# Wider W_in products, raw W_out blocks stored in batch 0, and one common form for the stretch between batches

## The chip, the cores and the metric

The kernel runs on one core of one Trainium2 chip. The metric is the device time of one execution in microseconds (us). Every profile here is one execution taken by the hardware profiler.

Engines: PE is TensorE (matmuls), PEld its weight loads, DVE is VectorE, ACT is ScalarE, POOL is GpSimd, SP is SyncE, which here only issues transfers (its queue is called SPq in the rows).

## What is computed

```python
def attn(x, state):                    # x [8,8,512,64], state [8,8,32,64]
    scores  = softmax(x @ state.T / 8)     # over the 32 states
    xread   = scores @ state               # [8,8,512,64]
    scores2 = softmax(state @ x.T / 8)     # over the 512 tokens
    sread   = scores2 @ x                  # [8,8,32,64]
    return concat([xread, sread], axis=2)  # 544 rows per batch and head
def moe(x, w_in, w_out):               # x [8*544, 512], w_in [512,2048], w_out [2048,512]
    h = x @ w_in
    g = where(h >= 1, h, where(h <= -1, 0, (h + 1)**2 / 4))
    return g @ w_out
```

## The kernel before

**The algebra.** `xread @ W_in` is `a @ (state @ W_in)`, so for each batch b the kernel first multiplies the states by W_in and then the softmax `a` by that product. W_in and W_out lie in eight chunks c or j of 256 hidden columns. Batches 0 to 7 are the 512 tokens of each batch, "batch 8" is the 256 state rows of all batches together. Each batch runs over steps (b, j), j = 0 to 7; a step makes the hidden values of chunk j and adds the product of the step before to the output sums.

**Precision.** Matmuls of the hidden values run in a reduced format. Each operand is held as a high part (written by ACT) and a low remainder (written by DVE), and three products of parts are summed. The small products `state @ W_in` (line 457, tiles `sw`), the scores (line 234, `sc`) and the read of the tokens (line 408, `sr`) are in plain float32. `rest(b, c)` splits one `sw` product: ACT copies the high part, DVE subtracts (line 1242).

**Batch 0** is ordered by hand in `SEQ`, a list per engine; `Plan` turns the lists into an emission order. In it the weights arrive, are decoded (`low`, `high`, `join`), and W_out is split into `wo[c]` (`part_high`, `part_low`). For c = 3 and up the joined W_out chunk `wf` is also stored to DRAM as `flat` from POOL's queue (line 891). `wf` has two buffers (tag `tmp`), so the next `join` into one waits until the `flat` of that buffer has landed and its split has read it.

**Batch 1** runs in `direct`, with 24 output matmuls of 512 columns per step on four PSUM banks `acc`. Beside it the kernel prepares the seven-product form that batches 2 to 7 use for `g @ W_out`: `fold_whole(c)` stores raw quadrants of `wo[c]` to the DRAM tile `fold` with three transfers from SP (lines 644 to 646) and gets the whole chunk again (an addition on POOL, or a load of `flat`); `fold_sums`, `fold_high` and `fold_low` make sums of quadrants, which go to DRAM from POOL. `load_wide(b, c)` brings both sets back as `wd`.

**The stretch between batches** lies in step (b, 0): the read of batch b's tokens (`read2`, needs the softmax tile `e2` and the tokens `xn`), four `sw` products for chunks (1,2), (3,4), (5,6) and (7, next batch's 0), and the scores of batch b+1. Batch 1 has its own form, `stretch`: its products stand in other PSUM tiles (`mm`, then three on `acc`), the scores wait for the `mm` tile, and the scores stay in PSUM while the softmax of batch 2 is worked on in halves. Batches 2 to 7 use `stretch_between`: `sr` on `acc`, products on `h`, `mm`, `acc`, `acc`, scores on `acc`, parked at once in SBUF by two ACT copies (`park_all`).

**Softmax by columns.** `shuffle` transposes `e2` by way of DRAM (`moved`): one store, then four loads back. Up to batch 2 it is issued from SP.

**Queues.** SP and POOL issue transfers in program order; a transfer that waits for a buffer holds up all behind it on that queue. `later(place, b, j, ...)` puts work at a named place of a step; in the steps of batch 1 the places come in the order half, low, mid, end, last.

Of the kernel before, what the change touches and what calls it, by code (L numbers as in the profile page):

```python
# [8 lines left out]
F32 = mybir.dt.float32  # L9
# [11 lines left out]
NG = 0  # L21
HALVES = (0,)
SPILL = 3
SEQ = {
# [76 lines left out]
def state_exchange_moe(  # L101
# [17 lines left out]
    nc = tc.nc  # L119
    B, P, NT, H, D = x.shape  # L120
    S = NT * P
    NS = 32
    DM = H * D
    NPR = H // 2
# [46 lines left out]

    sb = const.tile([P, B, NPR, NS], F32, name="sb")
    srT = const.tile([P, NPR, B, NS], F32, name="srT")
    w32 = [const.tile([P, NPR, CI], F32, name=f"w32_{c}") for c in range(NC)]
    wo = {}
    rows2 = drams.tile([B, P, P], F32, tag="rows2", bufs=1, name="rows2")

# [267 lines left out]
    def sw_product(items, apart=None, home=None, halves=False):  # L445

        b, c = items[0]
        if apart:
            banks = [apart(f"sw{b}_{c}_{hh}") for hh in range(2)]
        else:  # L450
            pt = ps_mm(f"sw{b}_{c}")
            banks = [pt[:, hh] for hh in range(2)]
        for i, (bi, ci) in enumerate(items):
            for pr in range(NPR):
                for hh in range(2):
                    rows = slice(hh * 64, hh * 64 + 64)
                    nc.tensor.matmul(  # L457
                        banks[hh][pr * NS:(pr + 1) * NS, i * CI:(i + 1) * CI],
                        lhsT=sb[rows, bi, pr], rhs=w32[ci][rows, pr], start=True, stop=True,
                    )  # L460
        w = len(items) * CI
        if b == 0 and c < NH:
            whole = work.tile([P, 1024], F32, tag="wh", name=f"sw{b}_{c}w").rearrange("p (q f) -> p q f", q=2)[:, :, :w]
            sw_of[b, c] = [(banks[q][:, :w], whole[:, q], None) for q in range(2)]
            chunk[b, c] = whole, None
            return
        wh, wl = (
            v[:, :2 * w].rearrange("p (q f) -> p q f", q=2) for v in split_tiles(f"sw{b}_{c}", home)
        )
        if apart or halves:  # L470
            sw_of[b, c] = [(banks[q][:, :w], wh[:, q], wl[:, q]) for q in range(2)]
        else:
            sw_of[b, c] = [(pt[:, :, :w], wh, wl)]
        for i, item in enumerate(items):
            cols = slice(i * CI, (i + 1) * CI)
            chunk[item] = wh[:, :, cols], wl[:, :, cols]
# [151 lines left out]
    fold = {}  # L628
    flat = {}

    def fold_whole(c):

        w = wo[c]
        wa = (wop if c >= SPILL else rawp).tile([P, 8, 256], F32, tag="wo" if c >= SPILL else "raw", name=f"wa{c}")
        fold[c] = wa
        hi, lo = (w[:, i].rearrange("p a c -> p (a c)") for i in range(2))
        whole = wa[:, 0:4].rearrange("p a c -> p (a c)")
        if c >= SPILL:
            nc.gpsimd.dma_start(out=whole, in_=flat[c])
        else:  # L640
            nc.gpsimd.tensor_tensor(out=whole, in0=hi.bitcast(F32), in1=lo.bitcast(F32), op=ALU.add)
        kept = folded[c] = drams.tile([P, 2, 8, 256], F32, tag="fold", name=f"fold{c}")
        w4 = w.bitcast(F32).rearrange("p i a (h c) -> p i (a h) c", h=2)
        nc.sync.dma_start(out=kept[:, :, 0:1], in_=w4[:, :, 0:1])
        nc.sync.dma_start(out=kept[:, :, 1:3], in_=w4[:, :, 2:4])
        nc.sync.dma_start(out=kept[:, :, 7:8], in_=w4[:, :, 1:2])

    def fold_sums(c):
        wa = fold[c]
# [265 lines left out]
    def part_low(c):  # L915
        wh, wl = (wo[c][:, i].rearrange("p a c -> p (a c)") for i in range(2))
        nc.vector.tensor_tensor(out=wl, in0=parts[c], in1=wh.bitcast(F32), op=ALU.subtract)

# [226 lines left out]
    def attention(b):  # L1145

        def at(place, j, *names):
            for name in names:
                f, *q = name.split()
                later(place, b - 1, j, (lambda f=f, q=q: getattr(atts[b], f)(*map(int, q)),))  # L1150

        if b == 2:
            at("mid", 1, "turn 0", "turn 1")
            at("low", 2, "top2 0", "top2 1")
            at("mid", 2, "top1 0", "top1 1")
            at("low", 3, "exp2 0", "exp2 1")
            at("mid", 3, "less1 0", "less1 1")
            at("low", 4, "exp1 0", "exp1 1", "turn_blocks 0")
            at("mid", 4, "sum1 0", "inv1 0")
            at("low", 5, "turn_blocks 1", "shuffle")  # L1160
            at("mid", 5, "sum1 1", "inv1 1", "norm1 0")
            at("low", 6, "norm1 1", "back 0")
            at("mid", 6, "back 1", "high1 0", "high1 1", "rest 0")
            at("low", 7, "rest 1")
            return
        at("f2", 1, "turn_all")
        at("f1", 2, "top2_all")
        at("f2", 2, "top1_all", "exp2 0")
        at("f0", 3, "exp2 1")
        at("f1", 3, "less1_all")  # L1170
        at("f2", 3, "exp1 0", "blocks_all")
        at("f0", 4, "exp1 1")
        at("f1", 4, "shuffle", "sum1_all")
        at("f2", 4, "norm1_all")
        at("f1", 5, "back_all")
        at("f2", 5, "high1 0")
        at("f0", 6, "high1 1")
        at("f1", 6, "rest_all")
# [28 lines left out]
    for c in range(2, NJ):  # L1207
        later("half", 1, c - 1, (fold_whole, c))
        later("low", 1, c, (fold_high, c - 1))
        later("mid", 1, c, (fold_low, c - 1))  # L1210
    later("end", 1, 2, (load_later, 0))
    later("mid", 1, 7, (one, 0, "read2", "scale2"))
    later("mid", 3, 5, (one, 0, "place2"))
    later("mid", 4, 5, (one, 1, "place2"))
# [4 lines left out]
    later("end", 1, 7, (fold_high, 7), (fold_low, 7))  # L1219
    for c in range(NG):  # L1220
        later("mid", 1, 0, (part_late, c))
    for c, (b, j) in enumerate(((1, 7), (1, 7), (1, 7))):
        later("last", b, j, (load_wide, 2, c))
    order = [s for s in steps if s[0] > 1]
    for i, s in enumerate(order[3:]):
# [15 lines left out]
            nc.scalar.copy(out=wh, in_=pt)  # L1241
            nc.vector.tensor_tensor(out=wl, in0=pt, in1=wh.bitcast(F32), op=ALU.subtract)  # L1242

    def stretch(b):
        atts[b].read2()
        sw_product([(b, 1), (b, 2)], halves=True)
        sw_product([(b, 3), (b, 4)], ps_acc)
        sw_product([(b, 5), (b, 6)], ps_acc, "xn")
        rest(b, 1)
        att_start(b + 1)  # L1250
        rest(b, 3)
        sw_product([(b, 7), (b + 1, 0)], ps_acc, "raw")
        atts[b].scale2()
        rest(b, 5)
        rest(b, 7)

    def stretch_between(b, now):

        final = b + 1 == B
        atts[b].read2(ps_acc)  # L1260
        atts[b].scale2()
        sw_product([(b, 1), (b, 2)], ps_h)
        rest(b, 1)
        if not final:
            att_start(b + 1, apart=ps_acc)
            atts[b + 1].park_all()
        now.last_sums()
        sw_product([(b, 3), (b, 4)])
        rest(b, 3)
        now.high(1)  # L1270
        now.low(1)
        now.high(2)
        sw_product([(b, 5), (b, 6)], ps_acc, "xn")
        rest(b, 5)
        now.low(2)
        sw_product([(b, 7), (b + 1, 0)][:1 if final else 2], ps_acc, "raw")

    def direct(b, j, prior):
        hid = g1(b, j, split=False)
# [18 lines left out]
    def sevenfold(b, j, prior, before):  # L1298
        now = Seven(b, j)
        old = before if before else None  # L1300
        gather = Gather(prior[0]) if old and j == 0 else None
        first = j == 0 and b < B
        late = old and old.b < B and old.j > 0
        now.product(0)
        now.curve(0)
        if late:
            old.high(2)
        now.bound(0)
        issue("curved", b, j)
        now.first_sum()  # L1310
        if late:
            old.low(2)
        issue("f0", b, j)
        now.high(0)
        now.low(0)
        issue("f1", b, j)
        if old:
            old.outer(0)
        else:
            g2(*prior, 0)  # L1320
        if gather:
            gather.keep(1)
            gather.keep(7)
            gather.add(2)
        issue("mid", b, j)
        now.product(1)
        now.curve(1)
        if old:
            old.outer(1)
        else:  # L1330
            g2(*prior, 1)
        if gather:
            gather.add(6)
            gather.keep(4)
        now.bound(1)
        if gather:
            gather.add(5)
            gather.keep(3)
            joins(gather, b)
        if first:  # L1340
            stretch_between(b, now)
        else:
            now.high(1)
            now.last_sums()
            now.low(1)
            issue("f2", b, j)
        return now
# [28 lines left out]
    with guard:  # L1376
        plan.emit(warm)
        before = None
        for i, (b, j) in enumerate(steps):
# [8 lines left out]
            if j == 1 and b + 2 < B:  # L1388
                loaded["xt", b + 2] = load_xt(b + 2)
            issue("end", b, j)  # L1390
            if j == 6 and b + 1 < B:
                loaded["xn", b + 1] = load_xn(b + 1)
            issue("last", b, j)
        g2(*steps[-1])
# [43 lines left out]
```

## Time and profile before

| | |
|---|---|
| median of 3 runs | 629.36 us (628.64 to 630.17) |
| profiled execution | 631.39 us, span of its work 629.5 us |
| busy, share of the span | PE 614.4 us (98%), DVE 499.3 (79%), ACT 464.4 (74%), POOL 66.4 (11%) |
| DMA | 178.05 MB, mean 283 GB/s |
| PE clock granted | full in all slices |

How to read it: the span runs from the first to the last instruction; the execution is 1.9 us longer. A matmul's end is modelled and overlaps the next one's start, so time on PE is best read from start to start. "Issue" as the releaser of a wait means that the profile shows no semaphore that the engine waited for.

### The profile page before, as it was taken

The numbers are of one execution on the slowest core, as the hardware profiler recorded it, in microseconds if no ns is written. First come the engines' busy times: TensorE is split into PE (matmuls) and PEld (weight loads), VectorE is DVE, ScalarE is ACT, GpSimd is POOL, SyncE is SP. The second block draws the span as 40 slices with busy tenths as digits, with TensorE's granted clock in tenths as the row PEclk, the third lists the DMA queues.
The fourth block names the chain that finished last, engine by engine and source line by source line (L and its number), as shares of the span: only waits on it lengthen the run. The fifth ranks groups of instructions, "written<-read, shape, count | busy, mean of one in ns | idle before, by whom it ended". The sixth has DMA issues, their size and how long they took to land.

```text
span 629.5 us, 12904 instructions
## 1 busy us (share of the span) xinstructions
PE 614.4 (98%) x5154; PEld 531.8 (84%) x5154; DVE 499.3 (79%) x765; ACT 464.4 (74%) x746; POOL 66.4 (11%) x85
## 2 busy tenths in 40 slices
PE   8999999999889999999999999999999999999997
PEld 3577776888679997999889998999899988999995
DVE  6999978799579878897789877997789777678631
ACT  6998855766478778787788777877878777777642
POOL 0000201211100101201120102010121011000200
PEclk9999999999999999999999999999999999999999
DMA  8993469869999987989698979999788978998741
GB/s 350 415 415 156 124 250 334 309 241 346 341 414 362 303 302 226 284 314 312 231 315 274 333 295 282 275 343 320 234 231 317 297 252 220 263 376 268 230 121 34
DMA packets 56715, 178.05 MB, mean 283 GB/s; under 512 B 9424, under 2 KB 25424, under 8 KB 53712
## 3 DMA queue, kind: packets, MB, share of 16 engines
q1 hardware_dynamic: 44240, 151.21, 67.2%
q0 software_dynamic: 12080, 25.69, 15.7%
q8 instruction: 41, 0.67, 0.4%
q10 hardware_dynamic: 336, 0.33, 0.2%
q14 instruction: 18, 0.15, 0.1%
HBM read 137.89 MB, written 33.03 MB: 272 GB/s over the span
## 4 chain that ended last, share of the span: by engine, by line
PE 75%; DVE 5%; DMA 4%; issue 2%; ACT 2%; SPq 1%; DVEq 0%; ACTq 0%
PE p L777 13%; PE p L779 13%; PE p L778 13%; PE h L708 7%; PE h L709 7%; PE h L710 7%; PE sw L457 4%; PE acc L612 2%; PE acc L610 2%; PE acc L611 2%; DMA moved<-eb 2%; PE h L523 2%; PE h L522 2%; PE h L524 2%; DMA fold<-wo 1%
## 5 line engine op out<-in xcount | busy, mean ns | idle before, releaser
L729 DVE SCALAR_TENSOR_TENSOR sums<-sums,over 128x512 f32<-128x512 f32 x96 | 65.9, 687 | 57.0 <-ACT sums L725 56.2
L777 PE MATMUL p<-wd,gh 128*128 128x256 f32 x384 | 108.5, 283 | 0.5 <-DVE sw_3l L1242 0.5
L778 PE MATMUL p<-wd,gh 128*128 128x256 f32 x384 | 108.7, 283 | 0.0
L779 PE MATMUL p<-wd,gl 128*128 128x256 f32 x384 | 108.6, 283 | 0.0
L750 ACT CAST gh<-sums 128x512 fp32r<-128x512 f32 x96 | 59.9, 624 | 57.6 <-DVE sums L729 33.3
L723 ACT ACTIVATE sums<-h,half 128x512 f32<-128x512 f32 x96 | 66.3, 691 | 25.7 <-PE h L710 24.2
L779 PE MATMUL p<-wd,gc 128*128 128x256 f32 x288 | 81.6, 283 | 0.0
L777 PE MATMUL p<-wd,gc 128*128 128x256 f32 x288 | 81.6, 283 | 0.0
L778 PE MATMUL p<-wd,gc 128*128 128x256 f32 x288 | 81.5, 283 | 0.0
L777 PEld LDWEIGHTS p<-wd,gh 128*128 128x128 f32 x384 | 72.9, 190 | 4.7 <-DVE sw_3l L1242 0.9
L778 PEld LDWEIGHTS p<-wd,gh 128*128 128x128 f32 x384 | 72.9, 190 | 3.8
L779 PEld LDWEIGHTS p<-wd,gl 128*128 128x128 f32 x384 | 72.9, 190 | 0.0
L754 DVE TENSOR_TENSOR gl<-sums,gh 128x512 fp32r<-128x512 f32 x96 | 65.8, 685 | 4.8 <-ACT gh L750 4.8
L724 ACT ACTIVATE over<-h,less_one 128x512 f32<-128x512 f32 x96 | 65.6, 684 | 0.0
L725 ACT ACTIVATE sums<-sums 128x512 f32<-128x512 f32 x96 | 60.8, 633 | 0.0
L777 PEld LDWEIGHTS p<-wd,gc 128*128 128x128 f32 x288 | 54.9, 191 | 0.0
L779 PEld LDWEIGHTS p<-wd,gc 128*128 128x128 f32 x288 | 54.9, 190 | 0.0
L778 PEld LDWEIGHTS p<-wd,gc 128*128 128x128 f32 x288 | 54.9, 191 | 0.0
L539 ACT ACTIVATE u<-h,half 128x512 f32<-128x512 f32 x40 | 27.0, 686 | 33.4 <-PE h L524 22.8
L612 PE MATMUL acc<-wo,gl 128*128 128x512 f32 x128 | 50.1, 391 | 0.5 <-DVE gl L572 0.5
L610 PE MATMUL acc<-wo,gh 128*128 128x512 f32 x128 | 50.2, 392 | 0.0
L611 PE MATMUL acc<-wo,gh 128*128 128x512 f32 x128 | 49.9, 390 | 0.0
(268 smaller groups left out, 1464.8 us busy)
## 6 DMA issues: line engine op xcount, KB each, us to landing
wd<-fold SPq DMA_DIRECT2D x96, 896.0 KB, 8.0
xt<-in_xt_dram SPq DMA_DIRECT2D x16, 512.0 KB, 8.3
raw_i<-in_moe_w_in_dram SPq DMA_DIRECT2D x8, 1024.0 KB, 9.6
raw_o<-in_moe_w_out_dram SPq DMA_DIRECT2D x8, 1024.0 KB, 12.3
out_dram<-o SPq DMA_DIRECT2D x32, 256.0 KB, 6.9
fold<-wa POOLq DMA_DIRECT2D x8, 1024.0 KB, 7.6
xn<-in_x_dram SPq DMA_DIRECT2D x7, 1024.0 KB, 6.1
fold<-wo SPq DMA_DIRECT2D x16, 256.0 KB, 6.6
```

The costliest lines, as they stand in the source:

```text
L610: nc.tensor.matmul(a, lhsT=lh, rhs=oh, start=f == 0, stop=False)
L611: nc.tensor.matmul(a, lhsT=lh, rhs=ol, start=False, stop=False)
L612: nc.tensor.matmul(a, lhsT=ll, rhs=oh, start=False, stop=f == NF - 1)
L723: nc.scalar.activation(out=g, in_=h, func=AF.Relu, scale=0.5, bias=half)
L724: nc.scalar.activation(out=r, in_=h, func=AF.Relu, scale=1.0, bias=less_one)
L725: nc.scalar.activation(out=g, in_=g, func=AF.Square)
L729: nc.vector.scalar_tensor_tensor(out=g, in0=g, scalar=1.0, in1=r, op0=ALU.min, op1=ALU.add)
L750: nc.scalar.copy(out=gh, in_=s)
L754: nc.vector.tensor_tensor(out=gl, in0=s, in1=gh.bitcast(F32), op=ALU.subtract)
L777: nc.tensor.matmul(o, lhsT=gh[:, sl], rhs=wh, start=opens, stop=False)
L778: nc.tensor.matmul(o, lhsT=gh[:, sl], rhs=wl, start=False, stop=False)
L779: nc.tensor.matmul(o, lhsT=gl[:, sl], rhs=wh, start=False, stop=closes)
```

## The change

1. Chunks 1 and 2, 3 and 4, 5 and 6 of W_in are kept in one tile per pair (`twins`). A product of two such chunks is then one matmul of 512 columns per head pair and half instead of two of 256.
2. The three transfers that store the raw quadrants of `wo[c]` become `keep_raw(c, queue)`. For c = 0 to 4 they are emitted in batch 0, behind `part_low(3)`, `part_low(4)` and `part_low(5)`, on POOL's queue. For c = 5 to 7 they stay in `fold_whole` on SP.
3. Batch 1's stretch takes the form of the later ones, and batch 2's softmax works on the parked scores in whole instructions, its `shuffle` at step (1,3) instead of (1,5).
4. The tokens `xn` of batch 2 are loaded into the `wh`/`wl` buffers at the end of step (1,4), not into `xn` at the end of (1,6).
5. The third pair of `wd` loads is emitted at the end of step (2,0) instead of (1,7).
6. In the last stretch (batch 7) `scale2` and `last_sums` come behind the split of chunks (3,4).

```diff
+RAW = {3: (0,), 4: (1, 2), 5: (3, 4)}
...
-    w32 = [const.tile([P, NPR, CI], F32, name=f"w32_{c}") for c in range(NC)]
+    w32 = [const.tile([P, NPR, CI], F32, name="w32_0")]
+    twins = {}
+    for c in range(1, NC - 1, 2):
+        twins[c] = const.tile([P, 2, NPR, CI], F32, name=f"w32_{c}")
+        w32 += [twins[c][:, i] for i in range(2)]
+    w32.append(const.tile([P, NPR, CI], F32, name=f"w32_{NC - 1}"))
...
+        if c in twins and len(items) == 2:
+            for pr in range(NPR):
+                for hh in range(2):
+                    rows = slice(hh * 64, hh * 64 + 64)
+                    nc.tensor.matmul(
+                        banks[hh][pr * NS:(pr + 1) * NS].rearrange("p (a f) -> p a f", a=2),
+                        lhsT=sb[rows, b, pr], rhs=twins[c][rows, :, pr], start=True, stop=True,
+                    )
...
+    def keep_raw(c, queue):
+
+        kept = folded[c] = drams.tile([P, 2, 8, 256], F32, tag="fold", name=f"fold{c}")
+        w4 = wo[c].bitcast(F32).rearrange("p i a (h c) -> p i (a h) c", h=2)
+        queue.dma_start(out=kept[:, :, 0:1], in_=w4[:, :, 0:1])
+        queue.dma_start(out=kept[:, :, 1:3], in_=w4[:, :, 2:4])
+        queue.dma_start(out=kept[:, :, 7:8], in_=w4[:, :, 1:2])
...
     def fold_whole(c):
 
+        if c not in folded:
+            keep_raw(c, nc.sync)
...
     def part_low(c):
...
+        for k in RAW.get(c, ()):
+            keep_raw(k, nc.gpsimd)
...
         if b == 2:
-            at("mid", 1, "turn 0", "turn 1")
-            at("low", 2, "top2 0", "top2 1")
-            at("mid", 2, "top1 0", "top1 1")
+            at("mid", 1, "turn_all")
+            at("low", 2, "top2_all")
+            at("mid", 2, "top1_all")
             at("low", 3, "exp2 0", "exp2 1")
-            at("mid", 3, "less1 0", "less1 1")
-            at("low", 4, "exp1 0", "exp1 1", "turn_blocks 0")
-            at("mid", 4, "sum1 0", "inv1 0")
-            at("low", 5, "turn_blocks 1", "shuffle")
-            at("mid", 5, "sum1 1", "inv1 1", "norm1 0")
-            at("low", 6, "norm1 1", "back 0")
-            at("mid", 6, "back 1", "high1 0", "high1 1", "rest 0")
-            at("low", 7, "rest 1")
+            at("mid", 3, "less1_all", "blocks_all", "shuffle")
+            at("low", 4, "exp1 0", "exp1 1")
+            at("mid", 4, "sum1_all")
+            at("low", 5, "norm1_all")
+            at("mid", 5, "back_all")
+            at("low", 6, "high1 0", "high1 1")
+            at("mid", 6, "rest_all")
             return
...
+    later("end", 1, 4, (load_later, 2))
...
-    for c, (b, j) in enumerate(((1, 7), (1, 7), (1, 7))):
+    for c, (b, j) in enumerate(((1, 7), (1, 7), (2, 0))):
...
+    def stretch(b, now=None):
 
         final = b + 1 == B
         atts[b].read2(ps_acc)
-        atts[b].scale2()
+        if not final:
+            atts[b].scale2()
         sw_product([(b, 1), (b, 2)], ps_h)
         rest(b, 1)
         if not final:
             att_start(b + 1, apart=ps_acc)
             atts[b + 1].park_all()
-        now.last_sums()
+            if now:
+                now.last_sums()
         sw_product([(b, 3), (b, 4)])
         rest(b, 3)
-        now.high(1)
-        now.low(1)
-        now.high(2)
+        if final:
+            atts[b].scale2()
+        if now:
+            now.high(1)
+            now.low(1)
+            if final:
+                now.last_sums()
+            now.high(2)
         sw_product([(b, 5), (b, 6)], ps_acc, "xn")
         rest(b, 5)
-        now.low(2)
+        if now:
+            now.low(2)
         sw_product([(b, 7), (b + 1, 0)][:1 if final else 2], ps_acc, "raw")
+        if not now:
+            rest(b, 7)
...
-            if j == 6 and b + 1 < B:
+            if j == 6 and 1 < b < B - 1:
                 loaded["xn", b + 1] = load_xn(b + 1)
```

## Rows read from the trace of the kernel before

**Rows 1.** The page: busy time, share of the span and instructions of each engine.

```profile
PE 614.4 (98%) x5154; PEld 531.8 (84%) x5154; DVE 499.3 (79%) x765; ACT 464.4 (74%) x746; POOL 66.4 (11%) x85
```

**Rows 2.** Waits of PE, whole span: us in total, times, longest.

```profile
PE sw L457 <- issue: 2.2, 2, 1.7
...
PE p L777 <- DVE sw_3l L1242: 0.5, 1, 0.5
PE acc L612 <- DVE gl L572: 0.5, 1, 0.5
```

**Rows 3.** Timeline of PE, batch 4's stretch: start, us, engine, line, operation, shapes, count.

```profile
310.39 1.10 PE L408 MATMUL sr<-xn,e 128*32 128x64 f32 x64
...
312.31 1.06 PE L234 MATMUL sc<-xt,sb 64*32 64x512 f32 x16
313.17 2.80 PE L457 MATMUL sw<-w,sb 64*32 64x256 f32 x96
315.89 0.50 PE L708 MATMUL h<-ath,sw_1h 128*128 128x512 f32 x1
```

**Rows 4.** Timeline of PE, batch 1's stretch; brackets: idle before, releaser.

```profile
93.88 1.10 PE L408 MATMUL sr<-xn,e 128*32 128x64 f32 x64
...
98.86 1.09 PE L234 MATMUL sc<-xt,sb 64*32 64x512 f32 x16 [1.13 <-issue]
...
101.03 0.50 PE L522 MATMUL h<-ath,sw_1h 128*128 128x512 f32 x1
```

**Rows 5.** Timeline of DVE in batch 1's stretch.

```profile
98.07 0.69 DVE L1242 TENSOR_TENSOR sw_1l<-sw,sw_1h 128x512 fp32r<-128x512 f32 x1 [0.65 <-ACT sw_1h L1241]
```

**Rows 6.** Timeline of PE, batch 2's stretch.

```profile
167.51 0.39 PE L612 MATMUL acc<-wo,gl 128*128 128x512 f32 x1
170.12 1.10 PE L408 MATMUL sr<-xn,e 128*32 128x64 f32 x64 [2.22 <-issue]
...
172.90 1.90 PE L457 MATMUL sw<-w,sb 64*32 64x256 f32 x55
176.46 1.50 PE L457 MATMUL sw<-w,sb 64*32 64x256 f32 x41 [1.66 <-issue]
177.89 0.50 PE L708 MATMUL h<-ath,sw_1h 128*128 128x512 f32 x1
```

**Rows 7.** Timeline of PE, batch 3's stretch.

```profile
240.79 1.10 PE L408 MATMUL sr<-xn,e 128*32 128x64 f32 x64
...
247.49 0.50 PE L708 MATMUL h<-ath,sw_1h 128*128 128x512 f32 x1
```

**Rows 8.** Tile xn, its issues from 159 to 163 us, and their time to landing.

```profile
L191 SPq DMA_DIRECT2D xn<-in_x_dram x1: 1108/1108/1108, 159.9 to 159.9; - x1
...
DMA to landing us min/median/max: 10.2/10.2/10.2
```

**Rows 9.** The page's DMA queues: packets, MB, share of 16 engines.

```profile
q8 instruction: 41, 0.67, 0.4%
```

**Rows 10.** Timeline of POOL in batch 0: its transfers of flat.

```profile
56.55 0.53 POOL L891 DMA_DIRECT2D flat<-wf  x1 [1.34 <-DVE wf L885]
68.93 0.53 POOL L891 DMA_DIRECT2D flat<-wf  x1 [11.84 <-DVE wf L885]
```

**Rows 11.** Tile flat, its issue at 68.93 us: time to landing.

```profile
DMA to landing us min/median/max: 3.7/3.7/3.7
```

**Rows 12.** Timeline of DVE: the last join of a W_out chunk.

```profile
73.40 1.22 DVE L885 SCALAR_TENSOR_TENSOR wf<-raw_o 128x1024 int32<-128x1024 int32 x1
```

**Rows 13.** Windows of 5 us: sum, busy PE, PEld, DVE, ACT, POOL; clock, DMA share, GB/s.

```profile
60.00:65.00 5.00, 5.00 (x23) 3.88 (x22) 5.00 (x7) 4.97 (x8) 0.00 (x0) 1.00 0.00 0
...
95.00:100.00 5.00, 3.87 (x114) 2.17 (x114) 3.17 (x7) 3.13 (x6) 0.00 (x0) 1.00 0.94 327
```

**Rows 14.** Tile fold, SP's issues of chunk 7's raw quadrants from 157 us, time to landing.

```profile
L644 SPq DMA_DIRECT2D fold<-wo x1: 518/518/518, 158.0 to 158.0; - x1
...
L646 SPq DMA_DIRECT2D fold<-wo x1: 632/632/632, 159.2 to 159.2; - x1
DMA to landing us min/median/max: 3.7/4.3/4.4
```

More of the change, by code (lines that the diff above doesn't have):

```diff
@@ L452, in sw_product @@
             banks = [pt[:, hh] for hh in range(2)]
-        for i, (bi, ci) in enumerate(items):
+        if c in twins and len(items) == 2:
[6 more added lines that the diff above has]
+                    )
+            items_left = []
+        else:
+            items_left = items
+        for i, (bi, ci) in enumerate(items_left):
             for pr in range(NPR):
@@ L641, in fold_whole @@
             nc.gpsimd.tensor_tensor(out=whole, in0=hi.bitcast(F32), in1=lo.bitcast(F32), op=ALU.add)
[L642 to L646, printed above, removed]
     def fold_sums(c):
@@ L1242, in rest @@
             nc.vector.tensor_tensor(out=wl, in0=pt, in1=wh.bitcast(F32), op=ALU.subtract)
[L1244 to L1252, printed above, removed]
-        atts[b].scale2()
-        rest(b, 5)
-        rest(b, 7)
-    def stretch_between(b, now):
+    def stretch(b, now=None):
         final = b + 1 == B
         atts[b].read2(ps_acc)
-        atts[b].scale2()
+        if not final:
+            atts[b].scale2()
         sw_product([(b, 1), (b, 2)], ps_h)
@@ L1340, in sevenfold @@
         if first:
-            stretch_between(b, now)
+            stretch(b, now)
         else:
```

## The prediction

> **What bounds the kernel now.** I read the page first: PE is busy for 98% of the span, the other engines for far less [rows 1], so only idle or stretched time of PE can be won. The waits of PE then say where it stands still: among them 2.2 us in two pauses inside `sw` products without a releaser, 0.5 us for a DVE split and 0.5 us for a `gl` in batch 0 [rows 2]. The timeline of PE, read stretch by stretch, gives prices, because batch 4's stretch runs without a pause and is a yardstick: 310.39 to 315.89, 5.50 us from the first `sr` to the next batch's first `h` [rows 3]. The same work takes 7.15 us in batch 1 (93.88 to 101.03) [rows 4], 7.77 us in batch 2 (170.12 to 177.89) after a wait of 2.22 us [rows 6], and 6.70 us in batch 3 (240.79 to 247.49) [rows 7]. Those excesses, 1.65, 2.22 + 2.27 and 1.20 us, are most of what the change can touch.
>
> **Batch 1's stretch in the later form.** `sc` starts at 98.86 [rows 4], just when DVE ends the second half of `sw_1l` (98.07 + 0.69 = 98.76) [rows 5]: the scores want the `mm` tile that `rest(1)` is emptying. In the new form they take two `acc` banks, which batch 0's output copies have emptied, and no product waits for a split that is not a whole product behind. The new waits (`sr` on `acc`, the first product on `h`) are for copies and bounds of work that PE did before; the park copies on ACT stand ahead of the last product's banks, with the time of two products between. What stands behind the stretch (the splits, `fold_high`, the next relu) moves forward with it. Gain: the excess, 1.65 us; bounds 0 (a bank is late) and 1.65.
>
> **Batch 2's tokens.** PE waits 2.22 us for `sr` with no semaphore named [rows 6], but `xn` was issued at 159.9 and took 10.2 us to land [rows 8], at 170.1, and `sr` starts at 170.12. So the transfer is what is late. It is now issued two steps earlier, into the `wh`/`wl` pair that chunks (3,4) leave. From 101.03 to 167.51 there are about eight steps [rows 4, 6], 8.3 us each (an estimate), so the tokens have some 16 us more. The order on SP's queue in batch 1 becomes: tokens of batch 0, store and four loads of batch 2's exchange, chunk 5's three raw transfers, store and four loads of batch 0's exchange, the two halves of batch 2's tokens, raw 6, raw 7, four `wd`. Each exchange holds the queue until its store lands, which costs the tokens a few of the 16 us. What is late next is nothing: after 167.51 the first `acc` bank has been copied and the exchange is long done. Gain 2.2 us; bounds 0 (PE then waits as long for the bound that empties the `h` bank, or for an output copy) and 2.22.
>
> **The pauses inside products.** In batch 2, PE stops for 1.66 us after 55 records of the last three products, 23 into a product of 32 [rows 6]. Nothing new is waited for there. The page has a queue of kind "instruction" with 41 packets, 0.67 MB [rows 9]; PE and PEld have 2 x 5154 instructions [rows 1], or 251 per packet. I take the pauses for instruction blocks that arrive late: a stretch has 64 `sr`, 128 `sw` and 16 `sc` records with as many weight loads, 416 instructions in 5.5 us, and crosses block borders far faster than the rest does. After the change three products of four have half the records: 320 instructions. At the pace of [rows 3], a block of 251 begun with `sr` lasts 1.92 (`sr` and the first product, 192 instructions) + 0.86 (`sc`, 32) + 0.38 (27 of 64) = 3.2 us before, and 1.92 (160) + 2 x 0.86 (64) + 0.7 (27 of 32) = 4.3 us after. That is 1.1 us more for the fetch: it covers batch 3's pause (2.2 - 1.7 = 0.5 us [rows 2]) and two thirds of batch 2's. There are fewer transfers in the way too, for five raw blocks, the tokens and one pair of `wd` leave that time. The excesses are 2.27 and 1.20 us together with the slow restart; I take three quarters of 3.47, or 2.6 us. Bounds 0 and 3.5.
>
> Here the Trainium skill speaks against the change: "Runtime: NRT & Kernel Launch", section "Instruction fetch mechanics", says that the sequencer refills its instruction memory in blocks of 16 KiB, 256 instructions, and that the cost of crossing a block is mostly hidden. The block size agrees with the 0.67 MB in 41 packets [rows 9]; by "mostly hidden" the pauses would have another cause, this term would be 0 and the time 625.5 us.
>
> **Wider products.** Three products of 256 columns take 315.89 - 313.17 = 2.72 us, 0.907 each, for 32 records; the scores, 16 records of 512 columns with the same 64x32 weights, take 313.17 - 312.31 = 0.86 [rows 3]. So PE streams the same columns either way, and 23 products (three in each of seven stretches, two in batch 0) can win 23 x 0.047 = 1.1 us at most, 0 at least. I take half, 0.5 us, since part of the 0.907 is the change of kind at the end.
>
> The skill's page "TensorE: Matmul & The Clock Gate", section "Wait — 56ns, not 53.3ns?", gives a floor of about 25 ns between matmul starts however small they are. The products run at 2.72 us / 96 = 28 ns per record [rows 3], near it; by that rule alone half the records would halve the product, but the 0.86 us of the scores speaks against it.
>
> **Last stretch.** PE waits 0.5 us for the split of chunks (3,4) [rows 2], which stands behind `scale2` and `last_sums` on DVE. Those go behind it: 0.5 us; bounds 0 and 0.5.
>
> **Raw blocks in batch 0.** Twelve transfers of chunks 1 to 4 follow the `flat` of chunk 4 (56.55) on POOL, at 0.53 us each [rows 10] issued by 63.5; then comes `flat` of chunk 7, at 68.93, when its join is done. None of the twelve waits for data. The engines are empty there (no bytes from 60 to 65 us) [rows 13], so they hide as long as they drain in time. But `flat` of chunk 7 is now behind them in the same queue, and DVE's last join, at 73.40 [rows 12], waits for its landing: 68.93 + 3.7 = 72.6 [rows 11], so there is 0.8 us to spare. Behind that join on DVE stand the bounds and the `gl` of step (0,6), for which PE waits already [rows 2]: each us that DVE is late there is one of PE. The four blocks have 4.2 MB; at 327 GB/s, a window in which raw blocks filled the engines [rows 13], they take 12.8 us, to 57.1 + 12.8 = 69.9. Then `flat` lands at 73.6, DVE is 0.2 us late, and batch 1's exchange store shares the engines. If they are gone before 68.93, which takes little more than that pace, the cost is 0. If the blocks don't overlap at all, each takes 159.2 + 4.4 - 158.0 = 5.6 us [rows 14]: 22.4 us, `flat` lands at 83.2, and DVE is 9.8 us late. I take 1.0 us lost, near the middle price. Chunk 0's three follow `flat` of chunk 3, where loads still run; what they take from these is in the upper bound.
>
> **Costed at nothing.** Parking adds two ACT copies and saves some DVE instructions in batch 1, where PE is at its pace throughout and ACT and DVE have gaps. `back_all` in (1,5) needs the buffer of batch 0's exchange, whose store is issued in (1,4): a step for it to land; if late, DVE's bounds wait. The third `wd` pair is used by PE in step (2,3), three steps after its new place.
>
> **Sum.** 1.65 + 2.2 + 2.6 + 0.5 + 0.5 - 1.0 = 6.45 us. On the profiled execution: 631.39 - 6.45 = 624.9, its span 623.1. The median of the runs lies 2.0 us under the profiled one; the same step from it gives 629.36 - 6.45 = **622.9 us**.
>
> **Rivals.**
> - *The pauses stay* (not fetched code, or the fetch is as late as before). For it: no view shows the fetch as releaser. Against: the place in mid-product. 622.9 + 2.6 = 625.5.
> - *`flat` of chunk 7 becomes the wait*, the one that ends on the other side. For it: 0.8 us to spare and 4.2 MB ahead in one queue. Against: empty engines. A drain of half way, 17 us, makes DVE 4.4 us late: 626.3. From 7.45 us late (a drain past 77.5 us) it is slower than before; at 9.8 us it gives 622.9 - 1.0 + 9.8 = 631.7.
> - *A new wait takes the place of the tokens'*: the park copies or the `h` bank in batch 1's or 2's stretch. Each would give back at most the term it stands in: 624 to 625.
> - *Products at half the time*: 23 x 0.43 (half of 0.86) = 9.9 us off, for 0.5 in the sum: 613.5. Only if the scores' pace is not theirs.
>
> **How the numbers follow.** Chances: the forecast 0.56 (its own range 621.2 to 624.2), pauses stay 0.17, `flat` late by some us 0.13 (0.05 of it by enough to be slower, 0.03 to come out level), a new wait 0.11, halved products 0.03. A run can tell 0.2% (1.3 us) from no change. Faster 0.90, same 0.04, slower 0.06 (with 0.01 for what I don't see). All gains at their bounds and no cost give 629.36 - 9.0 = 620.4. The range reaches to the pauses that stay and a half-late `flat`, 620.8 to 626.6.
>
> **What would show it.** Right: batch 1's stretch near 5.5 us with `sc` directly behind a product; `sr` of batch 2 directly behind the last `acc` matmul; no PE wait without a releaser in batches 2 and 3; a product of 16 records at 0.86 us; L777 without its wait in the last stretch. Wrong: PE waiting for `gl` around 80 us longer than 0.5 us with DVE's last join behind a late `flat`; pauses of 1 us and more inside the stretches; DVE held at `back_all`.

## The result, and the profile after

The changed kernel takes 633.48 us (median of nine runs, 631.71 to 636.31), the kernel before 630.17 beside it (nine runs, 627.25 to 631.32). The ratio is 1.0059, with a 95% interval of 1.0037 to 1.0081: the change makes the kernel slower by 0.6%. The forecast was 622.9 us.

The profiled execution of the changed kernel is the quickest of its nine (631.71, span 629.9), and that of the kernel before one of the longer ones (631.39, span 629.5); set against each other they show only 0.3 us of the 3.3, and the other 3.0 lie in the spread of runs, which no trace here shows. But they show well where time went and came from.

The page of the changed kernel, busy time, and its instruction queue (queue, kind: packets, MB, share), against [rows 1, 9]:

```profile
PE 615.8 (98%) x4786; PEld 527.0 (84%) x4786; DVE 500.2 (79%) x752; ACT 464.8 (74%) x747; POOL 77.9 (12%) x100
...
q8 instruction: 38, 0.62, 0.4%
```

There are 368 matmuls and as many weight loads fewer, which is 23 products of 32 records halved. The instruction queue has three packets fewer. The timeline of PE of the changed kernel, the stretch of batch 1 against [rows 4], and those of batches 2 and 3 against [rows 6, 7]:

```profile
97.46 1.10 PE L414 MATMUL sr<-xn,e 128*32 128x64 f32 x64
98.49 1.09 PE L463 MATMUL sw<-w,sb 64*32 64x512 f32 x16
99.38 1.06 PE L240 MATMUL sc<-xt,sb 64*32 64x512 f32 x16
100.23 1.92 PE L463 MATMUL sw<-w,sb 64*32 64x512 f32 x32
101.95 1.07 PE L474 MATMUL sw<-w,sb 64*32 64x256 f32 x32
102.95 0.50 PE L539 MATMUL h<-ath,sw_1h 128*128 128x512 f32 x1
...
171.06 0.39 PE L629 MATMUL acc<-wo,gl 128*128 128x512 f32 x1
171.38 1.10 PE L414 MATMUL sr<-xn,e 128*32 128x64 f32 x64
...
176.87 0.50 PE L730 MATMUL h<-ath,sw_1h 128*128 128x512 f32 x1
...
239.75 1.10 PE L414 MATMUL sr<-xn,e 128*32 128x64 f32 x64
...
245.24 0.50 PE L730 MATMUL h<-ath,sw_1h 128*128 128x512 f32 x1
```

All three stretches now take 5.49 us, with no pause, and batch 2's `sr` follows its predecessor without a wait. These gains were forecast, at 1.65, 2.6 and 2.2 us; they measure 1.66 us in batch 1's stretch, 2.28 and 1.21 in those of batches 2 and 3, and 2.22 of wait, 7.4 in all. Yet batch 1's `sr` starts at 97.46 instead of 93.88, batch 3's is only 1.0 us earlier (239.75 against 240.79), and the last matmul ends later. The waits of PE in the changed kernel (total, times, longest) name the three places that gave the gain back:

```profile
PE h L539 <- DVE u L563: 3.1, 2, 2.5
PE sr L414 <- issue: 1.6, 1, 1.6
PE sw L474 <- DVE rs L422: 1.6, 1, 1.6
```

**Batch 0: the raw blocks delay the exchange.** The timelines of DVE and PE, and the tile `moved` (issue and time to landing), in the changed kernel:

```profile
62.02 0.70 DVE L390 STREAM_TRANSPOSE eb<-e 128x512 f32<-128x512 f32 x1
...
67.45 1.23 DVE L907 SCALAR_TENSOR_TENSOR wf<-raw_o 128x1024 int32<-128x1024 int32 x1
...
72.32 1.22 DVE L501 TENSOR_TENSOR sw_7l<-sw,sw_7h 128x1024 fp32r<-128x1024 f32 x1
76.82 1.23 DVE L907 SCALAR_TENSOR_TENSOR wf<-raw_o 128x1024 int32<-128x1024 int32 x1 [3.28 <-DMA moved<-eb]
```

```profile
76.45 0.39 PE L629 MATMUL acc<-wo,gl 128*128 128x512 f32 x1
79.29 0.61 PE L539 MATMUL h<-ath,sw_7h 128*128 128x512 f32 x1 [2.46 <-DVE u L563]
79.70 0.63 PE L540 MATMUL h<-ath,sw_7l 128*128 128x512 f32 x1
80.13 0.63 PE L541 MATMUL h<-atl,sw_7h 128*128 128x512 f32 x1
```

```profile
L399 SPq DMA_DIRECT2D moved<-eb x1: 330/330/330, 69.3 to 69.3; - x1
...
DMA to landing us min/median/max: 7.4/7.4/7.4
```

DVE's last join stood at 73.40 before [rows 12] and stands at 76.82 now, after 3.28 us of idle time. What it waits for is not `flat` of chunk 7 but batch 1's exchange store, issued at 69.33 as before; it took 7.4 us to land where it took 3.9. The reason lies in the buffers: the tag `tmp` has two, and it serves not only `wf` but also `eb`, the tile that the store reads. `eb` takes one at 62.02, the join of chunk 7 the other at 67.45, so the last join (of chunk 6) gets the buffer of `eb`. In the trace the join's semaphores include the one of the store and not the one of that `flat`, which landed at 75.8 (68.98 + 6.8), 1.0 us before the join started. So the description ahead, by which a join waits for the `flat` of its buffer, does not hold for this join.

Behind the join stands the bound (`u`, L563) that PE needs: PE waits 2.46 us. Then the matmuls start 0.43 us apart instead of 0.23: the granted clock is at 1.2 GHz for 3.41 us (from 79.5), which costs another 1.7.

**Step (1,7): batch 0's exchange.** The queue of SP and the timeline of PE in the changed kernel:

```profile
131.26 0.33 SPq L399 DMA_DIRECT2D moved<-eb  x1
134.95 2.65 SPq L403 DMA_DIRECT2D e<-moved  x4
137.65 0.62 SPq L652 DMA_DIRECT2D fold<-wo  x1
...
139.69 1.24 SPq L399 DMA_DIRECT2D moved<-eb  x1
147.84 2.15 SPq L403 DMA_DIRECT2D srT<-moved  x4
```

```profile
154.54 0.39 PE L541 MATMUL h<-atl,sw_7hl 128*128 128x512 f32 x1
156.53 1.10 PE L414 MATMUL sr<-xn,srT 128*32 128x64 f32 x64 [1.60 <-issue]
```

The second exchange store (139.69) lands 8.1 us later. The four loads of `srT` follow at 147.84 and take up to 7.2 us, and PE waits 1.60 us for them in the read of batch 0's first state. In the kernel before, the store of this exchange was issued at 136.06 and landed in 2.6 us, and PE did not wait there.

**The last stretch.** PE in the changed kernel:

```profile
516.23 0.59 PE L474 MATMUL sw<-w,sb 64*32 64x256 f32 x2
518.40 0.66 PE L474 MATMUL sw<-w,sb 64*32 64x256 f32 x14 [1.58 <-DVE rs L422]
518.99 0.50 PE L730 MATMUL h<-ath,sw_1h 128*128 128x512 f32 x1
...
519.79 0.57 PE L730 MATMUL h<-ath,sw_1h 128*128 128x512 f32 x1
520.16 0.63 PE L731 MATMUL h<-ath,sw_1l 128*128 128x512 f32 x1
```

The wait of 0.5 us for `sw_3l` [rows 2] is gone. But the last product needs the `acc` bank that `scale2` (rs, L422) frees, and `scale2` now stands behind two splits: PE waits 1.58 us, and again the granted clock is at 1.2 GHz for 3.41 us (from 519.9).

The account of the two profiled executions, from one first read (`sr`) to the next, in us (plus is time lost): up to batch 1's +3.58; on to batch 0's first state -0.03 (the stretch won 1.66, the wait lost 1.60); on to batch 3's -4.59; on to batch 4's -1.39; to batch 7's 0.0; to the start of the last matmul +2.94. The sum is +0.5.

### The profile page after: what moved, and what is told of

It is laid out like the page before. It is cut to its first block, busy times and chain, and to the rows that moved or that the text cites. A ratio compares the mean times of both kernels' runs of the same rounds, so it can differ in the third digit from the quotient of the medians.

```text
span 629.9 us, 12154 instructions
## 1 busy us (share of the span) xinstructions
PE 615.8 (98%) x4786; PEld 527.0 (84%) x4786; DVE 500.2 (79%) x752; ACT 464.8 (74%) x747; POOL 77.9 (12%) x100
## 4 chain that ended last, share of the span: by engine, by line
PE 85%; DVE 1%; DMA 1%; ACT 1%; issue 1%; DVEq 0%; ACTq 0%
PE p L801 13%; PE p L800 13%; PE p L799 13%; PE h L730 7%; PE h L731 7%; PE h L732 7%; PE acc L627 4%; PE acc L628 4%; PE acc L629 4%; PE sw L463 3%; PE h L540 3%; PE h L539 2%; PE h L541 2%; PE sr L414 1%; DMA moved<-eb 1%; PE sw L474 1%
## 5 line engine op out<-in xcount | busy, mean ns | idle before, releaser
L799 PEld LDWEIGHTS p<-wd,gh 128*128 128x128 f32 x384 | 73.8, 192 | 4.1
L800 PEld LDWEIGHTS p<-wd,gh 128*128 128x128 f32 x384 | 73.8, 192 | 3.7
```

Of the source, the lines that this page charges most:

```text
L799: nc.tensor.matmul(o, lhsT=gh[:, sl], rhs=wh, start=opens, stop=False)
L800: nc.tensor.matmul(o, lhsT=gh[:, sl], rhs=wl, start=False, stop=False)
```

## The experiments

In all of them the kernel before ran beside on the same chip (medians 629.6 to 630.8 us). Each time below is a median, with the ratio to the kernel before and its 95% interval in brackets.

**Do the raw blocks cost batch 0 its time?** Edit of the changed kernel:

```diff
-RAW = {3: (0,), 4: (1, 2), 5: (3, 4)}
+RAW = {}
```

> The changed kernel with all raw blocks stored in batch 1 from SP, as before. Theory (the raw blocks in batch 0 hold up batch 1's exchange store, DVE's last join starts at 76.8 instead of 73.4 us, PE idles 2.5 us and then runs 3.4 us at half its clock): the first read of batch 1 is back at about 93.9 us (97.5 in the changed kernel), the clock is full from 70 to 90 us, and some 3.6 us are won, 1 or 2 of which may go again to transfers that now stand in batch 1: about 630 to 631.5 us. Rival (the raw blocks are hidden, and the wide products or the new order bring the late join and the clock): first read still near 97.5 us, 633.5 us.

It takes 632.16 us, ratio 1.0023 [1.0005, 1.0041]. Batch 1's read is back at 93.70, at full clock, so the early raw blocks are shown to cost batch 0 its time. But most of the gain did not stay. PE in this run:

```profile
156.35 1.93 PE L414 MATMUL sr<-xn,srT 128*32 128x64 f32 x64 [5.19 <-issue]
```

The wait for batch 0's first state grew from 1.60 to 5.19 us, and the clock is at 1.2 GHz for 6.83 us (from 154.8): all the raw transfers stand in batch 1 again.

**What does the last stretch's order cost?** The changed kernel with `scale2` and `last_sums` of the last stretch where they stood before:

> The changed kernel with the last stretch in its old order (the scale of the read and the last sums ahead of the splits). Theory (the last product waits for the bank of the read, which the scale empties behind two splits: 1.6 us, and the clock then halves for 3.4 us, 1.7 us): no wait for rs, full clock from 510 to 530 us, the 0.5 us wait for the split of chunks (3,4) back: 2.8 us won, about 630.7 us. Rival (the clock falls for another reason, and the wait hides the old one): the window from 520 us still shows a lower clock, at most 1.1 us won.

It takes 631.47 us, 1.0016 [0.9999, 1.0033]: 2.0 us less than the changed kernel. From batch 7's first read to the start of the last matmul it takes 109.76 us, as before (109.73), against 112.67 in the changed kernel. So this part of the change is a loss and not the gain of 0.5 us.

**Is it the count of instructions that ends the pauses?** The changed kernel with the products back at 256 columns, all else kept:

```diff
-        if c in twins and len(items) == 2:
+        if False:
```

> The changed kernel with products of 256 columns (the pair tiles stay). Theory A (the pauses inside the products went because fewer instructions are fetched): pauses of about 0.5 to 2 us come back in the stretches of batches 2 and 3, each stretch is up to 1 us longer, 635 to 637 us. Theory B (they went because five raw blocks, the tokens and a wide load left that time): no pause, stretches of 5.5 us, 633.5 to 634.5 us.

It takes 633.63 us, 1.0046 [1.0029, 1.0063]. The pauses are back in batches 2 and 3 (PE's waits: total, times, longest), whose stretches take 7.95 and 6.76 us again:

```profile
PE sw L474 <- issue: 2.3, 2, 1.5
...
PE p L800 <- DMA wd<-fold: 1.5, 1, 1.5
```

Of the products only the number of instructions changed, and the pauses came back with it: that is theory A. The time, though, is the one that theory B expected. Part of the reason is in the trace, which shows no stretch at 1.2 GHz before the end, where the changed kernel's has two of 3.41 us; over their runs the mean granted clock is 0.996 to 1.0 here and 0.988 to 0.999 there. Against that stands a new wait in the second row: PE, held up less in batch 0 this time, runs into a late `wd`. That these make up for the pauses is argued and not tested.

**The raw blocks alone, on the kernel before.**

```diff
+RAW = {3: (0,), 4: (1, 2), 5: (3, 4)}
...
+        for k in RAW.get(c, ()):
+            keep_raw(k, nc.gpsimd)
```

> The kernel before with the raw blocks of chunks 0 to 4 stored in batch 0 from POOL, nothing else. Theory: batch 0 loses 3.6 us (first read of batch 1 near 97.4 us, lower clock around 80 us); by theory A the pauses in batches 2 and 3 stay and the time is 632.5 to 634 us; by theory B they go and it is 630 to 631 us. Rival (batch 0 is hurt by another part of the change): first read at 93.9 us.

It takes 633.72 us, 1.0058 [1.0037, 1.0079]: this part alone costs what the whole change costs. But not all of it is lost in batch 0. Batch 1's read comes at 96.17, 2.3 us late; the wait for the tokens of batch 2, which are still issued late here, is 3.45 us instead of 2.22, and 3.41 us at 1.2 GHz follow it.

**The repairs one by one.** Fewer raw blocks early (`5: (3, 4)` left out):

> The changed kernel with fewer raw blocks in batch 0: chunks 3 and 4 are folded as before (their block 0 or blocks 1 and 2 too), and only the raw blocks left over by them go early. Theory (the transfers of the raw blocks delay batch 0's exchange store, DVE's last join waits for it, batch 1 reads late): with fewer of them batch 1's first read is back near 93.8 us (97.46 in the changed kernel), its join no longer stands idle for 3.3 us, the clock is full at 80 us, and the time falls by some 3.6 us to about 630. Rival (the order of the exchanges and not the count of transfers makes it late): batch 1's read stays at 95 to 97 us and the time within 1 us of 633.5.

It takes 630.89 us, 1.0001 [0.9975, 1.0027]: 2.6 us less than the changed kernel. DVE's last join stands at 74.38 and no longer waits. Batch 1's read stands at 94.81; the 0.9 us against the kernel before were there already at 57.53, where `flat` of chunk 4 was issued (56.55 before), ahead of the raw blocks of chunks 1 and 2. What is left is a wait for `wd` in batch 2, as in the next runs. Batch 0's exchange ahead of batch 2's:

```diff
-            at("mid", 3, "less1_all", "blocks_all", "shuffle")
-            at("mid", 4, "sum1_all")
+            at("mid", 3, "less1_all")
+            at("mid", 4, "blocks_all", "shuffle", "sum1_all")
...
-    later("mid", 1, 4, (one, 0, "turn_blocks 1", "shuffle"))
+    later("mid", 1, 3, (one, 0, "turn_blocks 1", "shuffle"))
```

> The changed kernel with batch 0's exchange one step earlier, ahead of batch 2's on SP's queue. Theory (batch 0's store stands behind batch 2's exchange and the three transfers of raw 5, so the read of batch 0's first state waits 1.6 to 2.3 us, and the clock sometimes falls behind it): the wait is gone, 631 to 632 us. Rival (the traffic of raw 5 alone fills the queues): a wait of 1 us or more remains there and the time stays near 633.5.

It takes 634.73 us, 1.0066 [1.0043, 1.009]. The wait for the first state is gone (the read starts at 154.86 behind a matmul), but PE then waits 1.23 and 1.74 us for the weights (`wd`) of batch 2's first seven-way step, with 3.41 us at 1.2 GHz from 180.3 on. The expected 631 to 632 us did not come. The second scaling alone back in front:

```diff
-        if not final:
-            atts[b].scale2()
+        atts[b].scale2()
...
-        if final:
-            atts[b].scale2()
```

> The changed kernel with the last stretch's second scaling back in front of the splits, and the sums still late. Theory (the last product needs the bank that this scaling frees, and it stands behind two splits): the wait of 1.58 us on rs is gone, and the half clock of 3.41 us behind it, and the wait of 0.5 us that the order before had does not come back; about 630.5 us. Rival (the late sums themselves hold the last product): a wait of over 1 us remains in the last stretch, and the time is within 1 us of 633.5.

It takes 633.55 us, 1.0044 [1.0028, 1.0061], as its rival expected. The wait on `rs` is gone, but the late `last_sums` hold the `gc` cast on ACT, which stands ahead of the cast of `sw_5h`: PE waits 1.25 us in the product behind, and 3.41 us at 1.2 GHz follow. Both halves of the new order cost. All three together:

> The three repairs together (fewer raw blocks early, batch 0's exchange ahead of batch 2's, the second scaling in front). Theory (three independent losses of 3.6, 1.6 to 2 and 1.6 to 2.8 us): about 625 us, faster than both kernels. Rival (one queue full throughout, so that a loss removed in one place comes back in the next): 629 to 632 us.

It takes 629.88 us, 0.9992 [0.9973, 1.0011]: the rival was right. In this run PE, the tile `wd` from 125 to 182 us, and windows of 5 us (length, busy PE, PEld, DVE, ACT, POOL; clock, DMA share, GB/s) show where the gain is lost:

```profile
175.00 0.36 PE L799 MATMUL p<-wd,gh 128*128 128x256 f32 x1 [1.26 <-DVE sw_5hl L1266]
177.11 0.46 PE L800 MATMUL p<-wd,gh 128*128 128x256 f32 x1 [1.75 <-DMA wd<-fold]
```

```profile
DMA to landing us min/median/max: 11.3/19.0/21.2
```

```profile
85.00:90.00 5.00, 5.00 (x23) 4.13 (x22) 2.95 (x5) 2.64 (x4) 0.00 (x0) 1.00 0.00 0
...
135.00:140.00 5.00, 5.00 (x24) 4.14 (x23) 4.93 (x9) 2.52 (x4) 1.23 (x2) 1.00 1.09 302
...
145.00:150.00 5.00, 5.00 (x24) 4.14 (x23) 3.81 (x7) 3.71 (x5) 1.23 (x2) 1.00 1.09 228
```

Both waits are for `wd`: its first two loads, issued at 155.3 and 155.9, land 19.6 and 21.2 us later, at 174.9 and 177.1, just ahead of the two matmuls. (The first row names a split on DVE, but in the fastest run below the same matmul starts at 174.22, ahead of that split's end.) The transfer engines are full from 135 us on; at 85 they stand empty. So the raw blocks cost at 57 to 65 us, and those sent from 98 to 150 stand ahead of `wd`; at 85 they would have the engines to themselves.

**The raw blocks where the engines are idle.** The run before with one line changed:

```diff
-    later("low", 1, 0, (fold_whole, 0))
+    later("low", 1, 0, (fold_whole, 0), *((keep_raw, c, nc.gpsimd) for c in range(3, NJ)))
```

> The three repairs, and the raw blocks of chunks 3 to 7 sent in batch 1's first step from POOL's queue (from some 78 us on), where the transfers of the three repairs' run were idle (share 0.00 from 85 to 90 us, 0.43 from 90 to 95) instead of at 98 to 150 us. Theory (with the waits ahead of it gone, the loads of batch 2's seven-way blocks are late at 175.0 and 177.1 us because the transfer engines stand at shares of 1.01 to 1.09 from 135 us on): these loads land some us earlier, the two waits of 1.26 and 1.75 us and the half clock of 3.41 us behind them are gone or small, and the time falls by 3 to 4.7 us to 625 to 627. Rival (these loads are late because they are issued late, at 155 us, behind waits of SP): the waits stay within 0.5 us and the time stays near 630.

It takes 626.87 us, 0.9947 [0.9927, 0.9967]. The median landing of `wd` falls from 19.0 to 8.7 us, and both waits and the stretch at 1.2 GHz are gone. Two things changed at once, though, and no run tells them apart. Without the raw blocks ahead on its queue, SP also issues the first `wd` 11 us earlier, at 144.3; with a landing of 19.6 us as before, even that would have been in time for its use at 175.1. And the transfer engines are as full as they were: a share of 1.02 from 135 to 155 and from 155 to 180 us, against 1.06 and 1.03 in the run before. So what went is the traffic ahead of the loads, while the engines stayed full. With the last stretch's old order:

> The same with the last stretch in the order of the kernel before. Theory (that order takes 109.7 us from its first read to the last product, in the kernel before and in the run that put it back, against 111.2 with the second scaling moved in front alone): another 1.5 us less, 623.5 to 625.5, faster than the kernel before by about 0.9%. Rival (a repair in one place comes back as a wait in the next): 628 to 630.

It takes 625.87 us, 0.9926 [0.9908, 0.9945], a little over the expected 623.5 to 625.5. And with batch 0's exchange behind batch 2's, as the change has it:

> The same as the run before it, with batch 0's exchange back behind batch 2's. Theory (the order of the two exchanges cost because raw 5's transfers and a full stretch stood there): with the raw blocks gone from there the wait for batch 0's first state is under 0.5 us and the time is that of the run before it within 1 us. Rival (the order itself costs): the wait of 1.6 to 2.3 us is back, and the time is 2 to 4 us above the run before it.

It takes 625.08 us, 0.9917 [0.9898, 0.9937], 0.8% faster than the kernel before. So the order of the exchanges costs nothing by itself; the traffic around them did. This kernel is the change with two edits: the raw blocks of chunks 3 to 7 go in batch 1's first step, from POOL's queue, and the last stretch is left as it was. The longest waits of PE in this run, two rows of its timelines (of PE and DVE), and its windows of 10 us:

```profile
PE warmed L164 <- POOL ident masks.py:199: 1.5, 1, 1.5
PE h L539 <- DVE u L563: 0.6, 1, 0.6
PE p L799 <- DVE sw_3l L1266: 0.5, 1, 0.5
PE acc L629 <- DVE gl L589: 0.5, 1, 0.5
```

```profile
174.22 0.28 PE L799 MATMUL p<-wd,gh 128*128 128x256 f32 x1
174.23 0.69 DVE L1266 TENSOR_TENSOR sw_5hl<-sw,sw_5hl 128x512 fp32r<-128x512 f32 x1
```

```profile
80.00:90.00 10.00, 9.51 (x43) 7.80 (x43) 7.77 (x14) 5.61 (x8) 6.78 (x11) 1.00 1.02 409
...
130.00:140.00 10.00, 10.00 (x46) 8.29 (x45) 8.74 (x16) 5.69 (x7) 2.48 (x4) 1.00 0.88 258
```

**Is it the place of the raw blocks alone?** The kernel before with the raw blocks sent as in the fastest run, and nothing else of the change:

> The kernel before with nothing of the change but raw blocks sent early, and these placed as in the fastest run so far: chunks 0 to 2 in batch 0, chunks 3 to 7 in batch 1's first step, all from POOL. Theory (the other parts of the change bring their part only through TensorE: pauses of 2.2 and 1.3 us, tokens' wait of 2.2 us, batch 1's 1.65 us): little of that is touched here, so the pauses in the stretches of batches 2 and 3 stay, and the time is 629 to 631, as before. Rival (the traffic alone makes the difference): 625 to 627, with the stretches of batches 2 and 3 at 6.7 us or longer still.

It takes 629.51 us, 0.999 [0.9974, 1.0006]: no change. The two pauses inside products are there, as its waits show:

```profile
PE sw L458 <- issue: 2.7, 2, 1.8
```

So the 5.7 us of the fastest run need other parts of the change, which the placement only lets through.

## Why the prediction was wrong

The time was missed by 10.6 us, and the sign with it. Three steps failed: the price of the raw blocks in batch 0 (1.0 lost in the sum, 3.58 in the trace), "what is late next is nothing" (1.60 lost), and the last stretch (0.5 won in the sum, 2.94 lost in the trace). Against the sum these are 2.6, 1.6 and 3.4 us. With the 0.5 of the wider products, and less the 0.9 that the stretches won beyond their terms, they come to 7.2 us; the two profiled executions miss the sum by 7.0, and the medians by 9.8, the rest of which is the spread named above. Step by step:

- *Batch 1's stretch* (1.65): right, 1.66 us.
- *Batch 2's tokens* (2.2): the wait is gone as said. The step "what is late next is nothing" failed: it asked only what stands behind the tokens in batch 2. It counted the exchange of batch 0, now behind batch 2's and chunk 5's raw transfers, as a few us for the tokens, and did not ask who waits for the loads of that exchange. PE waits 1.6 us for them, 2.3 in the run with the last stretch put back, and 5.2 with all raw blocks back there.
- *The pauses* (2.6): too small; 3.5 us, its upper bound. The narrow run brings them back with the instruction count. That late instruction blocks are behind it is not tested by itself, but the packets of the instruction queue in the traces speak for it. In the kernel before, the window from 174 to 175 us holds one of them:

```profile
q8 instruction: 1, 0.02, 6.0%
```

It ends at 174.99, in the pause of batch 2 (174.80 to 176.46). In the kernel before, the narrow run and the last run, each of the six pauses inside a product ends 1.3 to 1.5 us after the end of such a packet, whether the pause is 0.6 or 1.8 us long. The Trainium skill's sentence in "Runtime: NRT & Kernel Launch", section "Instruction fetch mechanics", that crossing a block is mostly hidden, is not what these runs show: there are pauses of 0.9 and 1.5 us at 416 instructions in a stretch in the narrow run, and none at 320 in the changed kernel and the fastest run.
- *Wider products* (0.5): nothing. Batch 4's stretch takes 307.96 to 313.45, 5.49 us against 5.50 [rows 3]. In batch 1's rows above, two wide products take 1.72 us and the narrow third, with the change of kind behind it, 1.00: 2.72 as before. The rival of products at half the time fell with it: 16 wide records take 0.86 us.
- *Last stretch* (0.5): wrong. The step looked at who waits for the split that moves forward and not at who waits for what moves back: the last product's bank behind `scale2`, and ACT's `gc` cast behind `last_sums`. Between medians the old order is worth 2.0 us. From batch 7's first read to the last matmul the new order takes 2.9 us more in the changed kernel, 1.2 GHz included, and 2.0 to 2.1 more in the runs with no raw blocks early, with three and with the exchange first, where the same wait of 1.58 us left the clock at 2.4 GHz.
- *Raw blocks in batch 0* (1.0 lost): batch 1's read came 3.58 us late, and the part alone costs 4.0 us between medians (633.72 against 629.77). The place was right, DVE's last join, but the wait was not: the join needs the buffer of `eb` and so the landing of the exchange store, which the text saw only as sharing the engines. In the kernel before this store landed at 73.1 (69.28 + 3.9), so the join at 73.40 had 0.3 us to spare and not 0.8. The last raw transfer, put at 69.9 in the sum, landed at 74.3 (64.59 + 9.7), near the half-way drain of the rival; in the 7.4 us of the store it and `flat` were under way too. (The drain past which the sum gives no gain is 73.4 + 7.45 - 3.7 = 77.2, not 77.5.)
- *Costed at nothing*: what comes late in the repaired runs is not the third `wd` pair, which was moved, but the loads that PE needs first, as soon as PE arrives early. The trace of the kernel before has the transfer engines at shares of 1.05, 0.99, 1.02 and 1.02 in the four windows of 10 us from 140 to 180 us. The text read the share at 60 and at 95 us only [rows 13], and not where the tokens, the exchange and `wd` go.
- The stretches at 1.2 GHz behind the new waits, 1.7 us for each 3.41 in which PE is busy, were in no term.

The sum also leaned on one execution. The tokens' wait of 2.22 us was read from a run 1.2 us above the median measured later. In the last experiment's trace that wait is gone too (`sr` of batch 2 at 168.07, directly behind `acc`; its tokens land at 161.3, with fewer raw blocks ahead of them), and yet its median is that of the kernel before. Both speak for a shorter wait in most runs of the kernel before; this is not shown, since one execution of each kernel is profiled.

## What to carry to other kernels

A transfer that nobody waits for still has a price: what shares the engines or the queue with it lands later. Before moving one, list what stands behind it on its queue and who waits for that, and read the transfer share over the whole stretch between its old and its new place. Then put it where the share reads near 0. Here raw blocks cost 4 us when they went at 57 to 65 us, held up other loads at 98 to 150, and left no long wait behind when they went from 78 us on. For a wait on a buffer, look up every tile that shares the buffer's tag, and not only the tile in question. When an order is swapped on one engine, look up who waits for the one that goes back, not only for the one that comes forward.

## What the runs showed of the hardware

- Around a wait of PE the granted clock often fell to 1.2 GHz for 3.41 us, once 6.83: with waits of 2.46 and 1.58 us (changed kernel), 5.19 (no raw blocks early), 2.26 (last stretch put back) and 3.45 (raw blocks alone). It did not with waits of 1.60 us in the changed kernel, 1.57 in the narrow run, and 2.22 and 1.66 [rows 6] in the kernel before. The same wait of 1.58 us in the last stretch came with a fall in the changed kernel and with none in three other runs. What decides it stays open. It is part of the spread of runs: the mean clock over the nine runs of the changed kernel goes from 0.988 to 0.999.
- Batch 1's exchange store, issued at 69.3, took 3.9 us to land in the kernel before, where the transfer share read 0.00 from 65 to 70 us and 0.63 from 70 to 75, and 7.4 in the changed kernel, at shares of 1.01 and 0.86. Later stores took 8.1 us at a share of 1.07 (changed kernel, 140 to 150) and, in the kernel before, 2.6 when issued at 136.06 and 11.1 when issued at 144.08 (1.05 from 140 to 150).
- The `wd` loads of 0.9 MB took 19.0 us at the median with raw blocks sent from 98 to 150 us and 8.7 without, though the share was 1.0 in both; what was already under way when they were issued differed.
